# Sliding-window attention with a gated feed-forward layer: stages of batches 2 and 3 grouped in three bursts a unit, first loads, first casts and weight loads in another order

## The chip, the cores and the metric

The kernel runs on one core of one Trainium2 chip. The metric is the device time of one execution in microseconds (us); below it is given as the median of 13 runs. A profile of one execution stands beside it.

## The reference, cut to what matters

There are 4 batches, 8 heads, 768 positions, head size 64, all inputs in float32.

```python
scores = q @ k.transpose(0, 1, 3, 2) / sqrt(64)
keep = (pos_k < 4) | ((pos_q - pos_k >= 0) & (pos_q - pos_k < 128))   # 4 sinks, window of 128
a = softmax(where(keep, scores, -1e9))
x = (a @ v).transpose(0, 2, 1, 3).reshape(3072, 512)
out = (maximum(x @ w_gate, 0) * (x @ w_val)) @ w_out     # d_model 512, d_ff 1536
```

## The kernel before, in words

**Units.** Attention is done in 16 units (U0 to U15), each a pair of heads of one batch: four units to a batch. A unit loads k, q and v in float32 into one of four staging buffers (`stg`, `load_kq` L105, `load_v` L114: one DMA for k, one for q, three for v, 5 in all, some 1.2 MB), casts them to bfloat16 (`cast` L124, on GpSimd), and transposes k and q so that the head size lies on the partitions. For batches 0 and 1 TensorE does this (`T`, L140) and ScalarE copies the results out of PSUM (L153); for batches 2 and 3 two DMAs on SyncE's queue do it (`X`, L134). `sinkk` (L155) has VectorE build a second copy of some keys (`kTs`) with the four sinks in front.

Scores come in three groups (`S`, L167), each followed by an exp on ScalarE (L183) and, for batches 1 to 3, a multiplication by a mask on VectorE (L185). Batch 0 has the mask added by a matmul of a bias instead (L174). Sums and outputs come in two halves (`norm`, L253): matmuls (`V`, L187, L201), then on VectorE a transpose, a reciprocal, a transpose and a product that writes `xT` (L260 to L265). Half 0 needs score groups 0 and 1, half 1 needs groups 1 and 2.

**The feed-forward layer** goes over 96 chunks (`chunk`, L270): a batch, a half of its positions (384) and one of 12 slices of d_ff. A chunk has four gate matmuls (gp, L275), a Relu on ScalarE (L278), four value matmuls (vp, L281) and a product on VectorE (L283). When the 12 slices of a half are done, 3 x 12 matmuls with `wo` (`ffn2`, L294) are queued in `f2`; up to three of them follow each later chunk. Twelve of them make a tile that ScalarE copies (L298) and SyncE's queue stores.

**The order is written out by hand.** `unit_stages` (L360) makes six stages of a unit x: `s(0)` (with `X` of unit x+1), `v` (half 1 of unit x-1), `s(1)`, `t`, `s(2)`, and half 0 of x. Stage `t` transposes the next unit (`T`) where TensorE does it, calls `sinkk` for it, issues weight loads on GpSimd's queue and the loads of unit x+5 or x+3 on SyncE's, and casts unit x+3 on GpSimd. `held` (L328) has VectorE write one element of the staging buffer first, so that the load waits until VectorE comes there. `PLAN` (L414) says how many stages stand ahead of which chunk: 28 ahead of chunk 0, then up to 50 by chunk 24, 74 by chunk 48, 98 by chunk 71. So from chunk 24 on there is one stage ahead of about every chunk.

**Queues.** Each engine executes in the order written. GpSimd's casts and its weight loads (`load_w` L207 for gate and value, four pieces each, `load_wo` L213, three pieces of four d_ff slices) are in one line: a weight load is issued only after the casts ahead of it, and those wait for their data. SyncE's queue holds the loads of k, q, v, the transposes `X` and the stores, in the order written. The three pieces of `wo` are issued in stage `t` of units 5, 6 and 7, ahead of the casts of U8, U9 and U10.

**Buffers.** Chunks and early attention take their PSUM tiles from a pool of three (`ps_gv`), scores and later outputs from a pool of two (`ps_at`).

**The beginning** (L334 to L355): SyncE's queue gets k of U0, v of U0, then U1, U2, U3, U4; q of U0 goes to ScalarE's queue. VectorE writes the bias (`setup_m0`) and, after the cast of U0's q, `setup_m1`. GpSimd casts k and v of U0, then k, q, v of U1, U2; stage `t` of U0 issues the first weight pieces ahead of U3's casts.

Of the kernel before, what the change touches and what calls it, by code (L numbers as in the profile page):

```python
# [33 lines left out]
def kernel(  # L34
# [12 lines left out]
    nc = tc.nc  # L47
    B, H, S, D = q.shape
    assert (B, H, S, D) == (4, 8, 768, 64)
    NP = H // 2  # L50
# [21 lines left out]
    kT = [const.tile([128, 872], BF16, name=f"kT{i}") for i in range(2)]  # L72
# [15 lines left out]
    class Unit:  # L88
# [34 lines left out]

        def cast(self, what, eng):  # L124

            if what in "kq":
                eng.tensor_copy((self.kn if what == "k" else self.qn)[:],  # L127
                                self.staging(what).rearrange("p h (n d) -> p n h d", d=64))
                return
            eng.tensor_copy(self.vn[:, 0:6, :, :], self.staging("v")[:, 0:6, :, :])  # L130
            eng.tensor_copy(self.vn[0:24, 6, :, :], self.staging("v")[0:24, 6, :, :])
            eng.tensor_copy(self.vn[0:4, 1:6:2, :, :], bc(self.vn[0:4, 0, :, :], 3))
# [7 lines left out]
        def T(self, first):  # L140

            s = self.s
            if first:
                ps = ps_gv.tile([128, 1024], BF16, name="tk", tag="gv")[:]
                pq = ps_op.tile([128, 1024], BF16, name="tq", tag="op")[:]
            else:
                both = ps_at.tile([128, 2, 1024], BF16, name="tkq", tag="at")
                ps, pq = both[:, 0, :], both[:, 1, :]
            for x, p_ in ((self.kn, ps), (self.qn, pq)):
                for t in range(6):  # L150
                    nc.tensor.transpose(p_[:, t * 128:(t + 1) * 128], x[:, t, :, :].rearrange("p h d -> p (h d)"), ident[:])  # L151
            for p_, dst, cp in ((ps, kT[s], nc.scalar.copy), (pq, qT[s], nc.scalar.copy)):
                cp(dst[:, 0:S].rearrange("d (p n) -> d p n", n=6), p_[:, 0:S].rearrange("d (n p) -> d p n", n=6))  # L153

        def sinkk(self):  # L155

# [61 lines left out]
    def setup_pool():  # L218
        make_identity(nc, ident)
        t0, a = bias[:, 0:255], bias[:, 503:754]  # L220
        for x, w, d in ((t0, 255, 0), (a, 251, 4)):
            nc.gpsimd.memset(x, 0.0)
            nc.gpsimd.affine_select(out=x, in_=x, compare_op=Alu.is_ge, fill=NEG, base=d,
                                    pattern=[[1, w]], channel_multiplier=-1)
            nc.gpsimd.affine_select(out=x, in_=x, compare_op=Alu.is_ge, fill=NEG, base=127 - d,
                                    pattern=[[-1, w]], channel_multiplier=1)
# [1 line left out]
    def setup_slot(s):  # L228
        nc.vector.memset(kT[s][:, S:872], 0.0)

    cp, ms = nc.vector.tensor_copy, nc.vector.memset

    def setup_m0():

        ms(bias[0:4, 0:128], 0.0)
        ms(bias[0:4, 128:255], NEG)
        cp(bias[:, 255:503], bias[:, 503:751])
        ms(bias[0:4, 255:503], 0.0)
        ms(bias[0:4, 503:627], NEG)

    def setup_m1():

        band, sk = (lambda a, b: bias[:, 503 + a:503 + b]), (lambda n: bias[:, 255:255 + n])
        cp(bias[:, 754:1002], sk(248))
        cp(bias[:, 1002:1253], band(0, 251))
        cp(bias[:, 1253:1397], sk(144))
        cp(bias[:, 1397:1417], band(0, 20))
        nc.vector.tensor_scalar(out=msk[:], in0=bias[:], scalar1=-1.0, scalar2=None, op0=Alu.is_ge)
# [53 lines left out]
    with tc.manual_schedule():  # L302
        U = [Unit(i) for i in range(B * NP)]
        on_array = []

        def at(x):
            return U[x] if 0 <= x < len(U) else None

        def casts(u, what, eng=nc.gpsimd):
            for w in what:  # L310
                u.cast(w, eng)

        warm_ps = []

        def warm(n):

            if not warm_ps:
                warm_ps.append(ps_at.tile([128, 2, 512], F32, name="warm", tag="at"))
            for _ in range(n):
                nc.tensor.matmul(out=warm_ps[0][:, 0, 0:128], lhsT=ident[:], rhs=ident[:], start=True, stop=True,  # L320
                                 skip_group_check=True)

        def load(x):
            U[x].load_kq("k", nc.sync)
            U[x].load_kq("q", nc.sync)
            U[x].load_v(nc.sync)

        def held(x):  # L328

            if x < len(U):  # L330
                nc.vector.memset(U[x].stg[0:1, 0:1], 0.0)
                load(x)

        U[0].load_kq("k", nc.sync)  # L334
        U[0].load_kq("q", nc.scalar)
        U[0].load_v(nc.sync)
        for x in range(1, 4):
            load(x)
        nc.vector.memset(ones[:], 1.0)
        setup_pool()  # L340
        nc.scalar.activation(ee[0][:, 0, 0, 0:64], ones[:], Act.Exp, bias=0.0, scale=1.0)
        for x in range(4):
            nc.vector.memset(vn[x][:, 6, :, :], 0.0)
        setup_slot(0)
        setup_slot(1)
        setup_m0()

        warm(16)
        casts(U[0], "k")
        casts(U[0], "q", nc.vector)  # L350
        casts(U[0], "v")
        casts(U[1], "kqv")
        casts(U[2], "kqv")
        load(4)
        setup_m1()  # L355


        stages = []

        def unit_stages(x):  # L360
            u, prev, nxt = U[x], at(x - 1), at(x + 1)

            def s(gi):
                def f():
                    if gi == 0 and u.p == 0:
                        xTs[u.b] = xpool.tile([128, NP, S], BF16, name="xT")
                    if gi == 0 and nxt is not None and nxt.xbar:
                        nxt.X()
                    u.S(gi)
                return f  # L370

            def v():
                if prev is not None:
                    norm(prev, 1, ps_at if on_array else ps_gv)

            def t():
                if nxt is not None:
                    if not nxt.xbar:
                        nxt.T(not on_array)
                    nxt.sinkk()  # L380
                if x == 0:
                    load_w(0)
                    load(5)
                elif x == 1:
                    load_w(1)
                elif x == 3:
                    load_w(2)
                    load(6)
                elif x == 4:
                    load_w(3)  # L390
                    load(7)
                elif 5 <= x:
                    held(x + 3)
                    if x < 8:
                        load_wo(x - 5)
                if at(x + 3) is not None:
                    casts(at(x + 3), "kqv")
            return [s(0), v, s(1), t, s(2), lambda: norm(u, 0, ps_at if on_array else ps_gv)]

        def first():  # L400
            U[0].T(True)
            U[0].sinkk()
        stages.append(first)
        for x in range(len(U)):
            stages += unit_stages(x)
        stages.append(lambda: norm(U[-1], 1))

        si = 0
        f2 = deque()
        total = len(stages)  # L410

        ORDER = [(0, h, m) for g in range(0, FM, 3) for h in range(2) for m in range(g, g + 3)]
        ORDER += [(b, h, m) for b in range(1, B) for h in range(2) for m in range(FM)]
        PLAN = ((0, 28), (24, 50), (48, 74), (71, 98))  # L414

        def want(ci):
            for (c0, w0), (c1, w1) in zip(PLAN, PLAN[1:]):
                if ci <= c1:
                    return w0 + (w1 - w0) * (ci - c0) // (c1 - c0)
            return total  # L420
        count = {}
        n = S // 2
        for ci, (b, h, m) in enumerate(ORDER):
            if b not in hTs:
                hTs[b] = hpool.tile([128, FM, S], BF16, name="hT", tag="hT")
            while si < min(total, want(ci)):
                stages[si]()
                si += 1
            if not ci:
                on_array.append(1)  # L430
            chunk(b, h * n, n, m)
            for _ in range(min(3, len(f2))):
                f2.popleft()()
            count[b, h] = count.get((b, h), 0) + 1
            if count[b, h] == FM:
                for t in range(3 * h, 3 * h + 3):
                    for mm in range(FM):
                        f2.append(lambda b=b, t=t, mm=mm: ffn2(b, t, mm, tail=b == B - 1))
        while f2:
            f2.popleft()()  # L440
# [33 lines left out]
```

The softmax here doesn't subtract the row's maximum and nothing guards it: scores larger than these inputs give would overflow.

## Time and profile before

| | |
|---|---|
| median of 13 runs | 266.36 us (263.61 to 269.73) |
| the profiled execution's own time | 266.07 us |
| its span, first to last instruction | 264.3 us |
| mean granted TensorE clock | 0.994 |
| TensorE matmuls busy | 252.1 us (95%) |
| VectorE busy | 147.4 us (56%) |
| ScalarE busy | 115.6 us (44%) |
| GpSimd busy | 62.7 us (24%) |
| moved by DMA | 33.54 MB |

PE is TensorE, DVE VectorE, ACT ScalarE, POOL GpSimd, SP SyncE; PEld are TensorE's weight loads, and a q behind a name is the engine's queue. Matmuls overlap, so their busy time says that TensorE is held, not that it is at its peak; the starting times of neighbouring matmuls tell the pace. A row of the timeline has the start, the time taken, the engine, the line and the operation; in brackets stands the idle time ahead of it and what ended it. The waits of an engine with slack cost nothing.

### The profile page before, as it was taken

To read this page: it belongs to the slowest core of one execution; us is meant where nothing else is said; L and a number is where in the kernel's file an instruction comes from. 1 tells how busy PE (TensorE), PEld (TensorE's weight loads), DVE (VectorE), ACT (ScalarE), POOL (GpSimd) and SP (SyncE) were. 2 spreads that over 40 slices of the span, in tenths; PEclk is the share of its full clock that TensorE was granted. 3 is DMA by queue.
4 is the path that set the end of the run, shared out by engine and by line. 5 is a ranking of instruction groups with operands and counts; after the bars stand their busy time and mean duration, and the time that the engine had idled before them with its cause. 6 is when DMAs were issued, how large, how long until landed. Compare 5 with 4: busy or idle time off the path is not lost.

```text
span 264.3 us, 5141 instructions
## 1 busy us (share of the span) xinstructions
PE 252.1 (95%) x1992; PEld 139.4 (53%) x1992; DVE 147.4 (56%) x318; ACT 115.6 (44%) x186; POOL 62.7 (24%) x102
## 2 busy tenths in 40 slices
PE   3999999999968999999999999999999999999994
PEld 3555655565534555555555555555565555555441
DVE  3399969778773566665647566575656232322100
ACT  2777855646423444344344434434433323333211
POOL 5787359072323141221305050000000000000000
PEclk9999999999997999999999999999999999999999
DMA  7999999998989393939559391311011011111132
GB/s 196 313 298 228 241 240 239 226 171 144 193 131 207 91 221 20 233 89 171 111 136 183 80 203 37 66 40 42 0 42 40 0 42 40 40 42 40 40 119 79
DMA packets 77318, 33.54 MB, mean 127 GB/s; under 512 B 64496, under 2 KB 74224, under 8 KB 77296
## 3 DMA queue, kind: packets, MB, share of 16 engines
q1 hardware_dynamic: 71216, 28.12, 47.2%
q0 software_dynamic: 5808, 4.72, 11.6%
q10 hardware_dynamic: 272, 0.39, 0.4%
q8 instruction: 15, 0.25, 0.4%
q14 instruction: 7, 0.06, 0.1%
HBM read 28.51 MB, written 6.29 MB: 132 GB/s over the span
## 4 chain that ended last, share of the span: by engine, by line
PE 78%; DMA 12%; SPq 6%; POOL 1%; issue 1%; ACT 1%; DVE 0%; POOLq 0%; ACTq 0%
PE gp L275 23%; PE op L294 23%; PE vp L281 21%; PE ops L201 6%; DMA stg<-in_v_dram 5%; DMA stg<-in_q_dram 5%; PE sps L179 4%; SPq L120 3%; DMA wo<-in_moe_w_out_dram 2%; SPq L112 2%; SPq L122 1%; PE tkq L151 1%; SPq L109 0%; POOL vn L130 0%; POOL qn L127 0%
## 5 line engine op out<-in xcount | busy, mean ns | idle before, releaser
L275 PE MATMUL gp<-xT,wg 128*128 128x384 bf16 x384 | 79.3, 330 | 0.0
L281 PE MATMUL vp<-xT,wv 128*128 128x384 bf16 x384 | 78.8, 328 | 0.3 <-DVE R L260 0.3
L278 ACT ACTIVATE gs<-gp 128x384 f32<-128x384 f32 x96 | 47.1, 490 | 72.6 <-PE gp L275 72.0
L294 PE MATMUL op<-wo,hT 128*128 128x512 bf16 x288 | 75.0, 381 | 2.7 <-DMA wo<-in_moe_w_out_dram 2.7
L283 DVE TENSOR_TENSOR hT<-gs,vp 128x384 bf16<-128x384 f32 x96 | 52.8, 552 | 42.7 <-PE vp L281 40.7
L183 ACT ACTIVATE ee<-sps 128x1006 bf16<-128x1006 f32 (+2 forms) x48 | 46.2, 964 | 38.8 <-PE sps L179 38.8
L281 PEld LDWEIGHTS <-wv 128*128 128x128 bf16 x384 | 37.8, 98 | 25.9 <-issue 1.5
L275 PEld LDWEIGHTS <-wg 128*128 128x128 bf16 x384 | 32.9, 98 | 27.3 <-issue 5.1
L294 PEld LDWEIGHTS <-hT 128*128 128x128 bf16 x288 | 28.3, 98 | 26.4 <-issue 0.6
L185 DVE TENSOR_TENSOR ee<-ee,msk 128x1006 bf16<-128x1006 bf16 (+2 forms) x36 | 26.0, 721 | 29.0 <-ACT ee L183 29.0
L127 POOL CAST kn<-stg 128x768 bf16<-128x768 f32 x16 | 13.3, 829 | 61.6 <-DMA stg<-in_k_dram 45.8
L298 ACT COPY ot<-op 128x512 f32<-128x512 f32 x24 | 14.1, 586 | 26.0 <-PE op L294 26.0
L260 DVE STREAM_TRANSPOSE R<-ops 128x384 f32<-128x384 f32 x24 | 13.9, 581 | 12.2 <-PE ops L201 12.1
L130 POOL CAST vn<-stg 128x768 bf16<-128x768 f32 x16 | 14.0, 873 | 23.3 <-DMA stg<-in_v_dram 21.1
L263 DVE STREAM_TRANSPOSE R<-rc 128x384 f32<-128x384 f32 x32 | 18.5, 578 | 1.1
L265 DVE TENSOR_TENSOR xT<-ops,R 128x384 bf16<-128x384 f32 x32 | 17.8, 557 | 1.7
L179 PEld LDWEIGHTS <-kT 64*128 64x128 bf16 x128 | 6.3, 93 | 22.5 <-issue 20.5
L201 PEld LDWEIGHTS <-ones 128*64 128x64 bf16 x288 | 12.3, 109 | 10.5 <-issue 7.5
L201 PE MATMUL ops<-ee,vn 128*64 128x255 bf16 (+8 forms) x288 | 15.5, 233 | 0.3 <-DVE xT L265 0.3
L179 PE MATMUL sps<-qT,kT 64*128 64x251 bf16 (+2 forms) x128 | 15.0, 255 | 0.1
L127 POOL CAST qn<-stg 128x768 bf16<-128x768 f32 x15 | 12.5, 836 | 8.6 <-DMA stg<-in_q_dram 7.9
L179 PE MATMUL sps<-qT,kTs 64*128 64x248 bf16 (+1 forms) x96 | 12.6, 259 | 0.4 <-DVE kTs L160 0.4
(53 smaller groups left out, 131.0 us busy)
## 6 DMA issues: line engine op xcount, KB each, us to landing
stg<-in_k_dram SPq DMA_DIRECT2D x16, 384.0 KB
stg<-in_v_dram SPq DMA_DIRECT2D x32, 192.0 KB
out_dram<-ot SPq DMA_DIRECT2D x24, 256.0 KB
stg<-in_q_dram SPq DMA_DIRECT2D x15, 384.0 KB
wg<-in_moe_w_gate_dram POOLq DMA_DIRECT2D x4, 384.0 KB, 8.3
wv<-in_moe_w_val_dram POOLq DMA_DIRECT2D x4, 384.0 KB, 10.4
wo<-in_moe_w_out_dram POOLq DMA_DIRECT2D x3, 512.0 KB, 7.1
stg<-in_q_dram ACTq DMA_DIRECT2D x1, 384.0 KB
```

The lines of the kernel that those rows point to most:

```text
L127: eng.tensor_copy((self.kn if what == "k" else self.qn)[:], self.staging(what).rearrange("p h (n d) -> p n h d", d=64))
L179: nc.tensor.matmul(out=ps[:, h, c:c + w], lhsT=self.kw(j, r), rhs=qT[s][r, qa:qa + w], start=not self.biased, stop=True, skip_group_check= ...
L183: nc.scalar.activation(x, ps[:, :, 0:c], Act.Exp, bias=0.0, scale=scale)
L185: nc.vector.tensor_tensor(x, x, bc(msk[:, m0:m0 + c], 2), op=Alu.mult)
L201: nc.tensor.matmul(out=ps[1 - what][64 * h:64 * h + 64, qa - q0:qa - q0 + w], lhsT=self.vn[:, j, h, :] if what else ones[:], rhs=ee[s][:, ...
L263: nc.vector.transpose(r[:, 1, 0:w], bass.AP(a.tensor, a.offset, [a.ap[0], [1, nb], [0, 32]]))
L265: nc.vector.tensor_tensor(xTs[u.b][:, u.p, c0:c0 + w], o[:, 0:w], r[:, 1, 0:w], op=Alu.mult)
L275: nc.tensor.matmul(out=gp[:, 0:n], lhsT=wg[:, ko, m * 128:(m + 1) * 128], rhs=x[:, ko, c0:c0 + n], start=ko == 0, stop=ko == KO - 1)
L278: nc.scalar.activation(gs[:, 0:n], gp[:, 0:n], Act.Relu, bias=0.0, scale=1.0)
L281: nc.tensor.matmul(out=vp[:, 0:n], lhsT=wv[:, ko, m * 128:(m + 1) * 128], rhs=x[:, ko, c0:c0 + n], start=ko == 0, stop=ko == KO - 1)
L283: nc.vector.tensor_tensor(hT[:, m, c0:c0 + n], gs[:, 0:n], vp[:, 0:n], op=Alu.mult)
L294: nc.tensor.matmul(out=op, lhsT=hTs[b][:, m, t * 128:(t + 1) * 128], rhs=wo[:, m, :], start=m == 0, stop=m == FM - 1)
```

## The change

1. `unit_stages`: for units 8 to 15 (batches 2 and 3) the six stages become three: `v` and `s(0)`; `t` and `s(1)`; half 0 and `s(2)`, each pair issued with no chunk between. `PLAN` counts 74 stages in place of 98, in the same stretches of chunks.
2. `load_wo`: the three pieces move one stage `t` ahead, to units 4, 5 and 6.
3. The first loads: k and q of U0 and U1, then v of both, all on SyncE's queue.
4. U0's k is cast by VectorE and its q by ScalarE; GpSimd begins with k and q of U1, then v of U0 and U1. U3's casts stand ahead of the first weight pieces.
5. In U0's `T` the copies of k go to VectorE, and both k and q are copied in two halves.
6. `setup_m0` goes to GpSimd, `setup_m1` behind U0's `sinkk`.

```diff
@@ cast
+            cp = eng.copy if eng is nc.scalar else eng.tensor_copy
...
@@ T
-            for p_, dst, cp in ((ps, kT[s], nc.scalar.copy), (pq, qT[s], nc.scalar.copy)):
-                cp(dst[:, 0:S].rearrange("d (p n) -> d p n", n=6), p_[:, 0:S].rearrange("d (n p) -> d p n", n=6))
+            for a, b in ((0, 64), (64, 128)) if self.i == 0 else ((0, 128),):
+                for p_, dst, cp in ((ps, kT[s], nc.vector.tensor_copy if self.i == 0 else nc.scalar.copy), (pq, qT[s], nc.scalar.copy)):
+                    cp(dst[:, 0:S].rearrange("d (p n) -> d p n", n=6)[:, a:b, :],
+                       p_[:, 0:S].rearrange("d (n p) -> d p n", n=6)[:, a:b, :])
...
-    cp, ms = nc.vector.tensor_copy, nc.vector.memset
     def setup_m0():
+        cp, ms = nc.gpsimd.tensor_copy, nc.gpsimd.memset
...
     def setup_m1():
+        cp = nc.vector.tensor_copy
...
-        U[0].load_kq("k", nc.sync)
-        U[0].load_kq("q", nc.scalar)
-        U[0].load_v(nc.sync)
-        for x in range(1, 4):
-            load(x)
+        for x in range(2):
+            U[x].load_kq("k", nc.sync)
+            U[x].load_kq("q", nc.sync)
+        for x in range(2):
+            U[x].load_v(nc.sync)
+        load(2)
+        load(3)
         nc.vector.memset(ones[:], 1.0)
         setup_pool()
+        setup_m0()
...
-        setup_m0()
         warm(16)
-        casts(U[0], "k")
-        casts(U[0], "q", nc.vector)
+        casts(U[0], "k", nc.vector)
+        casts(U[0], "q", nc.scalar)
+        casts(U[1], "kq")
         casts(U[0], "v")
-        casts(U[1], "kqv")
+        casts(U[1], "v")
         casts(U[2], "kqv")
         load(4)
-        setup_m1()
@@ stage t
+                if x == 0:
+                    casts(at(x + 3), "kqv")
                 if x == 0:
                     load_w(0)
                     load(5)
...
                 elif x == 4:
                     load_w(3)
                     load(7)
+                    load_wo(0)
                 elif 5 <= x:
                     held(x + 3)
-                    if x < 8:
-                        load_wo(x - 5)
-                if at(x + 3) is not None:
+                    if x < 7:
+                        load_wo(x - 4)
+                if x and at(x + 3) is not None:
                     casts(at(x + 3), "kqv")
-            return [s(0), v, s(1), t, s(2), lambda: norm(u, 0, ps_at if on_array else ps_gv)]
+            def v0():
+                norm(u, 0, ps_at if on_array else ps_gv)
+
+            def both(f, g):
+                return lambda: (f(), g())
+            if x < NP:
+                return [s(0), v, s(1), t, s(2), v0]
+            return [both(v, s(0)), both(t, s(1)), both(v0, s(2))] if x >= 8 else [s(0), v, s(1), t, s(2), v0]
         def first():
             U[0].T(True)
             U[0].sinkk()
+            setup_m1()
...
-        PLAN = ((0, 28), (24, 50), (48, 74), (71, 98))
+        PLAN = ((0, 28), (24, 50), (48, 62), (71, 74))
```

## The prediction

> **What bounds the kernel.** I read the slices first, then the chain of waits, then the timeline where TensorE is not dense.
>
> The page, the second part (span in 40 slices of 6.6 us):
>
> ```profile
> span 264.3 us, 5141 instructions
> ...
> PE   3999999999968999999999999999999999999994
> ...
> PEclk9999999999997999999999999999999999999999
> DMA  7999999998989393939559391311011011111132
> ```
>
> TensorE is held from the second slice to the last, but for slices 11 to 13 (70 to 85 us), where the granted clock dips too. DMA is busy in nearly every slice up to there. So the time is: the start of the dense part, plus TensorE's work, plus that one hole. The chain of waits agrees: from 35.39 us on it is matmuls but for one piece on `wo` (73.35 us, 6.60 us) and a few us ahead of it.
>
> The hole, from the timeline of 71.5 to 102 us:
>
> ```profile
> 72.75 0.33 DVE L159 COPY kTs<-kT 128x372 bf16<-128x372 bf16 x1 [1.50 <-DMA kT<-kn]
> ...
> 73.34 0.83 DVE L283 TENSOR_TENSOR hT<-gs,vp 128x384 bf16<-128x384 f32 x1
> 73.35 0.74 POOL L214 DMA_DIRECT2D wo<-in_moe_w_out_dram  x1
> ...
> 75.36 0.82 PE L275 MATMUL gp<-xT,wg 128*128 128x384 bf16 x4
> ...
> 76.67 0.59 PE L294 MATMUL op<-wo,hT 128*128 128x512 bf16 x2
> ...
> 79.99 0.38 PE L294 MATMUL op<-wo,hT 128*128 128x512 bf16 x1 [2.72 <-DMA wo<-in_moe_w_out_dram]
> ...
> 80.62 1.46 PE L275 MATMUL gp<-xT,wg 128*128 128x384 bf16 x4
> ...
> 88.85 0.81 PE L294 MATMUL op<-wo,hT 128*128 128x512 bf16 x3
> ...
> 90.80 0.81 PE L294 MATMUL op<-wo,hT 128*128 128x512 bf16 x3
> ...
> 91.54 0.28 PE L179 MATMUL sps<-qT,kT 64*128 64x251 bf16 x2
> ```
>
> The third piece of `wo` was issued at 73.35 and TensorE had to wait for it at 77.1; behind the wait matmuls take near twice their time. The first row is VectorE waiting for U8's transposed keys: it comes back below.
>
> **The sum is made against the profiled execution**, 266.07 us (span 264.3 and 1.8 around it), 0.29 below the median of the runs.
>
> **Part 1, `wo` one stage earlier.** Three output matmuls take 0.65 us (88.85 to 89.50, the next chunk's start), 0.216 each. The third of chunk 23 was due at 76.67 + 0.43 = 77.10 and came at 79.99: 2.89 us lost. From chunk 24's first gate matmul (80.62) to the next stage (84.34) 3.72 us pass, elsewhere 1.95 + 0.09: 1.68 us lost at the lower clock (0.78 granted from 76.5 to 84.4). Together 4.57 us. In the new order the third piece stands behind U8's casts. Those ended at 61.05 before; a piece took 6.6 us to land (73.35 to 79.95), so 67.7 and 9 us early, if nothing else moved.
>
> But it does move. Piece one now follows the fourth gate and value pieces (issued 43.29 to 44.8) at once, not U7's casts (55.50). In the timeline U7's v was asked for at 39.12 and its cast began at 54.04, after 7.67 us of waiting, while the third and fourth weight pieces were moving; U6's v, asked for at 33.29 mostly behind the first four, was there at 41.37. So a load of 256-byte rows nearly stands still beside a weight piece. With `wo` queued directly behind, U8's loads (asked for at 48.14, cast 56.24 to 60.4) meet two pieces of `wo` instead of one. That puts U8's last cast between 61 (the gaps are used: DMA share 0.75 from 54 to 57 us, 0.84 from 57 to 62) and 61 + 7; I take +7 or a little more, since those gaps are small. The third piece then lands at 75 to 77, about when it is due (77.10 less the earlier start, 76.2).
>
> **What is late next** is U8's keys. SyncE's queue holds U9's loads ahead of U8's transposes (issued 69.49 and 71.31 in before). VectorE waits in `sinkk` for them (72.75), and behind it in its line stands chunk 21's product, which ended at 74.17 and frees a PSUM buffer for chunk 23's gate at 75.36: 1.19 us of slack, 0.3 once the start is 0.9 earlier. If the keys land d later, TensorE stands d - 0.3. Bounds: d = 0 (gaps absorb the pieces) and d = 7.5 (a whole piece ahead of the transposes). I take 1.5, near the low end: U8's loads come later by a piece, but U9's, asked for at 61.17 and kept to 72.7 by the second piece, then run between two pieces. Cost 1.2. Net of part 1: -3.4 us.
>
> [...]
>
> **Part 2, three bursts a unit.** A stage after output matmuls starts 0.74 us after their first (90.80 to 91.54, and 93.14 to 93.88 for sums), a chunk 0.65. So entering a stage costs 0.09, and the first gate group after it 0.01 more (0.66 and 0.65). Leaving sums and outputs costs the same whatever follows:
>
> ```profile
> 99.40 0.51 PE L201 MATMUL ops<-ee,vn 128*64 128x119 bf16 x10
> 99.85 0.34 PE L275 MATMUL gp<-xT,wg 128*128 128x384 bf16 x1
> ```
>
> ```profile
> 19.88 0.51 PE L201 MATMUL ops<-ee,vn 128*64 128x119 bf16 x10
> 20.33 0.39 PE L174 MATMUL sps<-bias,ident 128*128 128x499 bf16 x1
> ```
>
> 0.45 us to a chunk's matmul (first fence) and to a score matmul (second, from the beginning, where they do follow each other). So a score group put behind outputs saves one entry, 0.10. Before there are 5 stages with matmuls a unit (`t` has none), 40 in all, the last two together; after, 3 a unit and one at the end, 25: 15 x 0.10 = 1.5 us. Bounds: nothing (a new wait for PSUM takes it) and 2.2. VectorE gets the four steps of a half (0.58 + 0.23 + 0.58 + 0.56) and a mask product (0.7) ahead of the chunk's product (0.55): 3.2 us from the burst's start, and the buffer it frees is wanted two chunks (3.9 us) later. ScalarE's exp (1.0) and Relu (0.5) are shorter. Both are covered; if not, a few tenths at 16 places. A chunk later than before the sums need their exp: score group 2 is now two chunks ahead of half 1 in place of three, 3.9 us for exp and mask of 1.5 and VectorE's 2.0.
>
> **Part 3, the beginning.** In before ScalarE copies U0's k (6.81, 0.80) and then q (7.51 to 8.31), scores start at 8.36 and the first exp at 9.07. After, q's cast is ScalarE's (0.8, by the row of its 768-wide copies, at 5.5 when q is there) and k's copy is VectorE's; the first score group needs only the first half of q's copy, and the bias matmuls (1.05) end at about 8.0. Gain 0.4 to 0.6. U1's k and q, cast behind U0's v at 8.75 to 10.34 before, now come first, so U1's transposes at 10.38 do not hold this up. From there ScalarE's line (1.0 + 1.0 + 0.9 exps, 1.6 copies of some 5.2 us a unit, 18.4 to 28.8) carries the 0.5 on. The setup on GpSimd lies in its 1.38 us of idleness ahead of 5.07; VectorE's `setup_m1` (1.3) ends some 0.5 ahead of the second bias matmul, and costs at most that if late.
>
> Then the dense part: TensorE waited at chunk 0's values (31.90), chunk 1's, and for U5's q (34.88), which had landed at 34.0 beside the first weight pieces:
>
> ```profile
> 31.90 0.81 PE L281 MATMUL vp<-xT,wv 128*128 128x384 bf16 x4 [0.27 <-DVE R L260]
> ...
> 34.00 0.83 POOL L127 CAST qn<-stg 128x768 bf16<-128x768 f32 x1 [1.34 <-DMA stg<-in_q_dram]
> ...
> 34.88 0.51 PE L151 MATMUL tkq<-ident,qn 128*128 128x128 bf16 x6 [0.30 <-POOL qn L127]
> ```
>
> Those pieces are now behind U3's casts. The v casts stood 4.0 apart (7.29, 11.22, 15.29), so U3's at 19.3, and 1.46 later the issue (20.62 to 22.08): 20.8 against 16.75. U4's and U5's k and q run ahead of them; the 0.46 of U5's q goes. But the values' piece, issued 0.87 later, lands 10.4 us on by the median: 32.1, or 31 with less beside it. Chunk 0's values want it at 31.4: 0 to 0.7 lost. Part 3 in all: -0.9, bounds -1.3 and +0.5.
>
> **Sum:** 266.07 - 3.4 - 1.5 - 0.9 = 260.3 us.
>
> **Rivals.**
> - *Nothing is late.* The pieces fill DMA's gaps and U8's keys keep their time: 266.07 - 4.57 - 1.5 - 0.9 = 259.1. For it: DMA moved 119 GB/s from 69 to 76.5 and 131 from 57 to 62, where 221 to 257 were seen before. Against it: U7's wait.
> - *The hole comes back at the keys.* d near 3.3, and a stand of 3.0 us is as long as the one that was followed by the low clock: 259.1 + 3.0 + 1.7 = 263.8. [...]
> - *The bursts give nothing*, because VectorE holds a buffer: 261.8. For it only that VectorE's work is bunched.
> - *Slower.* The third piece gets between U9's loads and U8's transposes: the keys land 7.5 late (80.3), TensorE stands 7.2 and then 1.7 at the low clock: 259.1 + 8.9 = 268.0. It is slower from keys at about 78.4 on. Against it: the piece waits for U8's casts, and U9's loads have to run slowly at that time too.
>
> **Chances.** Forecast (259.4 to 261.5) 0.48; nothing late 0.20; hole at the keys 0.16; bursts give nothing 0.09; slower 0.07. The range 258.0 to 264.0 takes in all but the slower case, the ends of the hole and the best of all bounds. Half a per cent, 1.3 us, is about what a measurement of this kernel can tell from no change; faster by more 0.89, within 0.04, slower by more 0.07.
>
> **What would show it.** TensorE's wait on `wo` gone or under 1 us; VectorE's wait for `kT` near 72 us longer than 1.50; clock near 1.00 from 76 to 85; a unit of batches 2 and 3 taking 14.5 us where the chain shows 14.68 (87.61 to 102.29); chunk 2's gate at 34.3 (35.23). Wrong if chunk 0's values wait over 1 us, if a wait for U8's keys passes 3 us, or if vp waits for VectorE appear after 85 us.

## The result and the profile after

The kernel after takes 262.46 us by the median of 11 runs (260.88 to 263.76), the kernel before 266.46 by that of the 48 runs beside it; the ratio is 0.9882 [0.9855, 0.9909]. The profiled execution took 262.48 us (span 260.7), so it stands for the median. The runs of one kernel spread over some us: of 29 runs of the kernel before, 7 have a granted clock of 1.00 and took 262.99 to 264.83, the other 22 have 0.987 to 0.994 and took 265.07 to 270.40; each stretch below is that of one execution.

The forecast was 260.3, and the time lies in its range; of the three parts, one went better than forecast, one nearly as forecast, and the third the other way. The starts of the chunks' first gate matmuls split the two spans into the same stretches (us; before, after, difference, forecast):

| stretch | before | after | difference | forecast |
|---|---|---|---|---|
| start to chunk 2 (part 3) | 35.23 | 37.32 | +2.09 | -0.9 |
| chunk 2 to 23 | 40.13 | 40.13 | 0 | 0 |
| chunk 23 to 26, the hole (part 1) | 12.18 | 7.53 | -4.65 | -3.4 |
| chunk 26 to 71 (part 2) | 110.57 | 109.40 | -1.17 | -1.5 |
| chunk 71 to the end | 66.18 | 66.33 | +0.15 | 0 |
| sum | 264.29 | 260.71 | -3.58 | -5.8 |

The page after, the span in 40 slices of 6.5 us:

```profile
span 260.7 us, 5138 instructions
...
PE   5998889999999999999999999999999999999994
...
PEclk9999799999999999999999999999999999999999
DMA  6899999998989976748391941311011101111132
```

The dip of the clock in slice 13 of the kernel before, with TensorE not full in slices 12 and 13, is gone. A new one stands in slice 5, with TensorE not full in slices 4 to 6.

**The hole.** TensorE's timeline (start, time taken, engine, line, operation, and in brackets the idle time ahead with what ended it):

```profile
76.00 0.81 PE L297 MATMUL op<-wo,hT 128*128 128x512 bf16 x3
...
78.76 0.81 PE L297 MATMUL op<-wo,hT 128*128 128x512 bf16 x3
...
80.66 0.82 PE L278 MATMUL gp<-xT,wg 128*128 128x384 bf16 x4
...
82.61 0.81 PE L278 MATMUL gp<-xT,wg 128*128 128x384 bf16 x4
```

No bracket is left and a chunk takes 1.95 us (80.66 to 82.61), where 3.72 passed before to the next stage. The third piece of `wo` landed at 74.38. VectorE's line at the same place, where I had put what is late next:

```profile
75.67 0.35 DVE L162 COPY kTs<-kT 128x372 bf16<-128x372 bf16 x1 [2.33 <-DMA kT<-kn]
...
76.28 0.54 DVE L286 TENSOR_TENSOR hT<-gs,vp 128x384 bf16<-128x384 f32 x1
```

U8's keys came 2.9 us later than before and VectorE waited longer (2.33, before 1.50), as forecast; but the whole kernel was 2.1 us later here, and the product behind the wait still freed its buffer in time for the gate at 77.45.

**A burst**, TensorE's timeline after 88 us:

```profile
88.24 0.81 PE L297 MATMUL op<-wo,hT 128*128 128x512 bf16 x3
88.98 0.47 PE L204 MATMUL ops<-ee,ones 128*64 128x255 bf16 x8
89.31 0.45 PE L204 MATMUL ops<-ee,vn 128*64 128x255 bf16 x8
89.69 0.28 PE L182 MATMUL sps<-qT,kT 64*128 64x251 bf16 x2
...
89.98 0.82 PE L278 MATMUL gp<-xT,wg 128*128 128x384 bf16 x4
```

The entry into the stage (0.74 for three `wo` matmuls instead of 0.65) is paid once for sums, outputs and scores; before, a score group had its own (the prediction's rows at 90.80 and 91.54). From chunk 24 (80.66) to chunk 30 (95.13) it is 14.47 us a unit, where the forecast said 14.5. No vp waits for VectorE after 85 us.

**The beginning.** TensorE's timeline, then the row of its weight loads, then GpSimd's:

```profile
26.99 0.51 PE L152 MATMUL tk<-ident,kn 128*128 128x128 bf16 x6 [1.55 <-POOL kn L128]
...
29.17 0.75 PE L204 MATMUL sums<-ee,ones 128*64 128x255 bf16 x8
...
32.77 0.81 PE L278 MATMUL gp<-xT,wg 128*128 128x384 bf16 x4 [0.19 <-DVE xT L268]
34.69 0.82 PE L284 MATMUL vp<-xT,wv 128*128 128x384 bf16 x4 [1.10 <-DVE R L266]
...
37.32 0.81 PE L278 MATMUL gp<-xT,wg 128*128 128x384 bf16 x4
```

```profile
34.69 0.28 PEld L284 LDWEIGHTS <-wv 128*128 128x128 bf16 x3 [1.49 <-DMA wv<-in_moe_w_val_dram]
```

```profile
21.54 0.83 POOL L131 CAST vn<-stg 128x768 bf16<-128x768 f32 x1 [0.55 <-DMA stg<-in_v_dram]
...
23.00 0.87 POOL L213 DMA_DIRECT2D wg<-in_moe_w_gate_dram  x1
23.87 0.75 POOL L213 DMA_DIRECT2D wv<-in_moe_w_val_dram  x1
...
25.33 0.77 POOL L213 DMA_DIRECT2D wv<-in_moe_w_val_dram  x1
26.06 0.87 POOL L128 CAST kn<-stg 128x768 bf16<-128x768 f32 x1
```

The same work of GpSimd in the kernel before:

```profile
16.75 0.87 POOL L210 DMA_DIRECT2D wg<-in_moe_w_gate_dram  x1
...
20.62 0.83 POOL L130 CAST vn<-stg 128x768 bf16<-128x768 f32 x1 [0.66 <-DMA stg<-in_v_dram]
...
23.55 0.84 POOL L127 CAST kn<-stg 128x768 bf16<-128x768 f32 x1
```

From the bottom up, in the kernel after: U3's v is cast at 21.54, the four weight pieces are issued behind it, and behind those stands the cast of U4's k, for which TensorE waits 1.55 us at 26.99 (0 before). The value piece issued at 23.87 lands at 34.64, and chunk 0's values wait for it. The matmul row names VectorE, which had read the sums by 33.80; the weight load's row names the DMA. The first exp does come earlier (8.03, before 9.07) and the lead holds to 23.86 (24.87), where these two waits take it.

DMA moved less early on. Windows of four us, of the kernel before and of the kernel after; the last three columns are the granted clock, the DMA share and GB/s:

```profile
8.00:12.00 4.00, 3.89 (x25) 1.94 (x24) 0.37 (x2) 2.83 (x4) 3.12 (x7) 1.00 1.17 300
```

```profile
8.00:12.00 4.00, 3.84 (x30) 1.84 (x30) 0.72 (x3) 3.52 (x5) 2.93 (x5) 1.00 0.79 164
...
28.00:32.00 4.00, 4.00 (x49) 2.62 (x48) 3.52 (x5) 2.76 (x4) 2.68 (x5) 0.57 1.24 189
```

The last row is the new dip: 0.57 of the clock for four us behind the stall, in which eight sums matmuls take 0.75 in place of 0.47.

### The profile page after: what moved, and what is told of

It is laid out like the page before. It is cut to its first block, busy times and chain, and to the rows that moved or that the text cites. A ratio compares the mean times of both kernels' runs of the same rounds, so it can differ in the third digit from the quotient of the medians.

```text
span 260.7 us, 5138 instructions
## 1 busy us (share of the span) xinstructions
PE 250.0 (96%) x1992; PEld 140.1 (54%) x1992; DVE 146.8 (56%) x315; ACT 116.2 (45%) x187; POOL 61.6 (24%) x106
## 4 chain that ended last, share of the span: by engine, by line
PE 88%; DMA 5%; DVE 2%; POOL 1%; ACT 1%; issue 1%; SPq 1%; ACTq 0%; DVEq 0%; POOLq 0%
PE gp L278 25%; PE vp L284 24%; PE op L297 24%; PE ops L204 7%; DMA stg<-in_q_dram 5%; PE sps L182 5%; PE tkq L152 1%; PE sps L177 1%; DVE kTs L163 1%; SPq L112 1%; PE tq L152 1%; DVE R L266 0%; ACT ee L186 0%; DVE R L263 0%; PE tk L152 0%
## 5 line engine op out<-in xcount | busy, mean ns | idle before, releaser
L278 PE MATMUL gp<-xT,wg 128*128 128x384 bf16 x384 | 78.5, 327 | 0.2 <-DVE xT L268 0.2
L278 PEld LDWEIGHTS <-wg 128*128 128x128 bf16 x384 | 34.0, 98 | 30.1 <-issue 4.9
L128 POOL CAST kn<-stg 128x768 bf16<-128x768 f32 x15 | 12.5, 831 | 53.1 <-DMA stg<-in_k_dram 30.4
L128 POOL CAST qn<-stg 128x768 bf16<-128x768 f32 x15 | 12.5, 831 | 11.3 <-DMA stg<-in_q_dram 10.4
L182 PEld LDWEIGHTS <-kT 64*128 64x128 bf16 x128 | 6.2, 94 | 13.6 <-issue 10.4
```

Source lines behind the costliest of these rows:

```text
L128: cp((self.kn if what == "k" else self.qn)[:], self.staging(what).rearrange("p h (n d) -> p n h d", d=64))
L182: nc.tensor.matmul(out=ps[:, h, c:c + w], lhsT=self.kw(j, r), rhs=qT[s][r, qa:qa + w], start=not self.biased, stop=True, skip_group_check= ...
L278: nc.tensor.matmul(out=gp[:, 0:n], lhsT=wg[:, ko, m * 128:(m + 1) * 128], rhs=x[:, ko, c0:c0 + n], start=ko == 0, stop=ko == KO - 1)
```

## The experiments

Two theories stood at first for the late beginning. G: GpSimd's line; U3's casts put ahead of the weight issues make these late, and U4's casts later still. L: the order of the loads; with k and q of two units first and then six v loads in a row DMA stands partly idle, and U2's and U3's v come late. Two runs check parts 1 and 2. All medians are of 6 to 12 runs; the kernel before took 266.6 to 267.1 beside them. Where the intervals of two ratios overlap, a difference is read from the timelines, each of one execution.

**1. The first weights ahead of U3's casts again** (all else as after).

```diff
                 if x == 0:
-                    casts(at(x + 3), "kqv")
-                if x == 0:
                     load_w(0)
...
-                if x and at(x + 3) is not None:
+                if at(x + 3) is not None:
```

> After, with U3's casts back behind the first weight pieces on GpSimd's queue. Theory G (GpSimd's line: U4's casts stand behind U3's v and four weight issues in a row, 23.00 to 26.06 us, so U4's transposes come 1.55 us late, the clock drops, and the first value piece lands only at 34.6): the wait for U4's k and the one for the value piece go, chunk 2's gate starts at about 34.3 us instead of 37.3, and the whole is about 259.5 us, unless U8's keys or wo now make TensorE stand around 76 us. Theory L (the load order: six loads of v in a row leave DMA partly idle from 9 to 12 us and bring U2's and U3's v 1 to 2 us later): U3's v still comes at 21.5, chunk 2's gate at 36.5 or later, the whole 261.5 or more.

263.76 us, ratio 0.9957 [0.9917, 0.9998]: slower than after. Chunk 0 comes at 30.58, as G had it, but chunk 2 only at 38.51. The profiled execution took 265.37, the longest of the twelve and 1.6 over their median, so the waits below are as long as they get; what is read from them is their order. GpSimd's rows, then TensorE's and SyncE's queue:

```profile
34.11 0.83 POOL L131 CAST vn<-stg 128x768 bf16<-128x768 f32 x1 [7.37 <-PE vp L284]
...
36.18 0.82 POOL L128 CAST kn<-stg 128x768 bf16<-128x768 f32 x1 [0.56 <-DMA stg<-in_k_dram]
```

```profile
37.06 0.51 PE L152 MATMUL tkq<-ident,kn 128*128 128x128 bf16 x6 [3.05 <-POOL kn L128]
```

```profile
20.79 4.20 SPq L112 DMA_DIRECT2D stg<-in_k_dram  x1
...
26.31 4.75 SPq L120 DMA_DIRECT2D stg<-in_v_dram  x2
```

The 7.37 us are put down to a matmul, but what came last is U4's v: asked for from 18.8 on, its pieces landed at 29.84, 33.97 and 34.39, beside four weight pieces whose parts landed from 23.6 to 35.6. U5's k, behind it in both lines, landed at 36.06. SyncE's queue sat 4.20 us on one issue and 4.75 on two. So the wait changes places: late weights make chunk 0's values wait, early ones U4's v and with it U5's k. Theory G alone falls.

**2. The loads in the order of before** (all else as after).

```diff
-        for x in range(2):
-            U[x].load_kq("k", nc.sync)
-            U[x].load_kq("q", nc.sync)
-        for x in range(2):
-            U[x].load_v(nc.sync)
-        load(2)
-        load(3)
+        U[0].load_kq("k", nc.sync)
+        U[0].load_kq("q", nc.scalar)
+        U[0].load_v(nc.sync)
+        for x in range(1, 4):
+            load(x)
```

> After, with the first loads in the order and on the queues of before (k of U0 and its v on SyncE's, q of U0 on ScalarE's, then unit by unit), the casts as in after. Theory L: U3's v is there at 19.3 instead of 21.5, U4's casts start 1.5 to 2 us earlier, chunk 2's gate at about 35, the whole about 260.5 us. Theory G: the four weight issues in a row still stand ahead of U4's casts and the value piece still comes late, chunk 2's gate at 36.5 or later, the whole 261.5 to 262.5; the first exp, at 8.03 in after, may be later by some tenths.

261.03 us, ratio 0.9862 [0.9808, 0.9916]. Chunk 2 at 35.90, 1.42 sooner than after; from 8 to 12 us DMA moves 300 GB/s again, U2's v is cast at 15.30 (17.94), U4's k at 25.09 (26.06), and no low clock is seen. Chunk 2 lies between L's 35 and G's 36.5. The ratio's interval overlaps that of the kernel after, so by time alone the gain isn't shown; run 9 against run 8 shows it again. GpSimd's row of U3's v:

```profile
20.56 0.83 POOL L131 CAST vn<-stg 128x768 bf16<-128x768 f32 x1 [2.14 <-DMA stg<-in_v_dram]
```

It comes at 20.56, as it did in before (20.62), though no weight piece stands ahead of it here.

**3. `wo` one stage earlier, alone** (the kernel before with the two lines of `load_wo` of the change).

> Before, with the three pieces of wo issued one stage earlier and nothing else. If the hole at 77 us was wo and the low clock behind it alone: the 4.6 us go and the whole is about 261.9 us (ratio 0.983). If U8's transposed keys are the next to be late when the start is not late too (in after they landed at 75.65 instead of 72.73, and the start came 2.1 later): TensorE stands 1 to 3 us at chunk 23 and the whole is 263 to 264.5.

262.20 us, ratio 0.9900 [0.9865, 0.9936]: part 1 alone gives as much as the whole change. The hole is gone (chunk 23 at 75.01, chunk 26 at 82.64: 7.63 us). VectorE's wait for the keys in this kernel:

```profile
73.56 0.31 DVE L159 COPY kTs<-kT 128x372 bf16<-128x372 bf16 x1 [2.66 <-DMA kT<-kn]
```

They came 0.8 later than before (72.75), within the 1.19 of slack, and TensorE did not stand. The granted clock is 0.997 or more in all twelve runs.

**4. After without the bursts** (`unit_stages` returns six stages, `PLAN` as before).

> After, with the six stages of a unit and the old plan for batches 2 and 3. If a merged stage saves one entry (0.1 us at 15 places): 1.2 to 1.5 us more than after, 263.6 to 264 us. If the bursts cost as much as they save by a new wait: the same as after, 262.5. The start and the stretch to chunk 23 stay as in after.

263.58 us, ratio 0.9952 [0.9908, 0.9997], 1.1 over after; chunk 26 to 71 takes 110.56, as before (110.57). So the bursts are worth 1.16 here, and nothing takes it. Another 0.10 of theirs lies in the stretch of the hole, 7.63 us in runs 3 and 4 and 7.53 in the kernel after.

**5. The base of the following runs.** In these, k and q of batches 2 and 3 are moved but not transposed.

```diff
-                nc.sync.dma_start_transpose(out=dst[:, 0:S].rearrange("d (t r) -> d t r", r=128),
-                                            in_=x[:].rearrange("r t h d -> r (t h d)"))
+                nc.sync.dma_start(out=dst[:, 0:S], in_=x[:].rearrange("r t h d -> r (t h d)"))
```

> The kernel after, but DMA carries k and q of batches 2 and 3 over as they lie, without transposing them (that part of the computation is left out; the DMAs, casts and waits keep their places). It is the base of the runs that have the same left out. Expected, since no wait for transposed keys stood on the path: the kernel after's course, chunk 2's first gate matmul at 37.3, chunk 26 at 85.0, in all 262.0 to 262.6 us. If it is faster by 0.5 us or more, the transposes cost time somewhere that the chain of waits did not name.

262.26 us, chunk 2 at 37.52: the course of the kernel after. What is left out does not carry its time. TensorE waits for U4's k here too, but the clock does not drop:

```profile
27.15 0.51 PE L151 MATMUL tk<-ident,kn 128*128 128x128 bf16 x6 [1.47 <-POOL kn L128]
```

```profile
28.00:32.00 4.00, 3.06 (x56) 2.23 (x58) 3.36 (x5) 2.77 (x4) 2.84 (x5) 1.00 1.25 191
```

The clock is 1.00 where the kernel after has 0.57, and chunk 2 comes no sooner (37.52, after 37.32). So the dip is not what makes the beginning late.

**6. The beginning of before, with the earlier `wo` and the bursts.**

> As the base (k and q of batches 2 and 3 not transposed), with the whole beginning of the kernel before; wo one stage earlier and the three bursts are kept. It prices the start edits by themselves. Theory 1 (they cost what the trace shows, 2.09 us at chunk 2, and nothing later gives it back): chunk 2 at 35.0 to 35.3, chunk 26 at 82.7 to 83.0, in all 1.4 to 2.1 us under the base. Theory 2 (a later wait takes the earlier start back): under 0.7 us.

260.81 us, by medians 1.45 under the base, as theory 1 had it. By the means of the six runs it is only 0.7, which is theory 2's, because two of them took 263. (One of these two was profiled, 263.45; in it U5's k and q made TensorE wait 1.18 and 0.83 us and chunk 2 came at 36.35.) So this run alone does not settle the price. Runs 3 and 4 do, with twelve runs each and the transposes in place: both have the earlier `wo` and no bursts, and they differ in the start edits alone. They took 262.20 and 263.58, so the start edits cost 1.4 us (by the means 1.4 too, give or take 0.6).

**7. Only the second pair of weight pieces one stage later.**

```diff
-                elif x == 1:
+                elif x == 2:
                     load_w(1)
```

> As the base, with one edit: the second pair of weight pieces one stage later. U4's k cast comes 1.5 us sooner (24.6 instead of 26.06). Theory G (U4's casts behind the issues make the late start, through the stall of TensorE and the low clock after it): transposes of U4 at 25.5 to 26, no dip of the clock, chunk 0 at 30.8 to 31.3, chunk 2 at 35.5 or sooner, 1.5 us or more under the base. Theory V (the values' piece alone sets it, since its issue stays at 23.9): the piece still lands at 34, or at 33 with nothing of the second pair beside it; chunk 0's values wait from 31.5 on, chunk 2 at 36.0 to 37.3, at most 1.2 us under the base.

263.08 us (262.4 without its two longest runs): no gain over the base, 262.26. U4's transposes came sooner (25.76), as G wanted, but the value piece, issued at 24.06, landed at 35.41 and chunk 0's values waited for it:

```profile
35.46 0.13 PEld L283 LDWEIGHTS <-wv 128*128 128x128 bf16 x2 [1.99 <-DMA wv<-in_moe_w_val_dram]
```

(The profiled execution took 265.07, one of the two longest, so only the order of events is read from it.) Theory V fits, by the time and by this order: the position of the first pair is enough to make the beginning late. With these few runs the time alone only just speaks against G's 1.5.

**8. Three edits together:** the loads of before (run 2), the first pair ahead of U3's casts (run 1), the second pair later (run 7).

> As the base, with three edits at the beginning: the loads in the order of before; the first pair of weight pieces issued ahead of U3's casts, as before; the second pair one stage later, ahead of U5's casts (its pieces are first wanted by chunk 6, near 42 us). Theory B (the beginning is bound by DMA bytes and by GpSimd's one line, and the second pair stands in both for nothing): the first pieces land by 29.5, chunk 0's values do not wait, U4's v and U5's k have no second pair beside them; chunk 0 at 30.0 to 30.6, chunk 2 at 33.8 to 34.6, in all 2.7 to 3.5 us under the base. Theory H (U5's casts now stand behind the second pair's issue, 1.5 us): the wait for U5's k goes on as in the run with w0 ahead, chunk 2 at 35.5 or later, under 1.8 us. If the second pair is late instead, chunk 6's gate waits for wg near 42 us.

259.46 us (259.07 to 259.91), ratio 0.9748 [0.9706, 0.9790], 2.8 under the base, as theory B had it. TensorE's timeline:

```profile
30.22 0.81 PE L277 MATMUL gp<-xT,wg 128*128 128x384 bf16 x4
31.31 0.81 PE L283 MATMUL vp<-xT,wv 128*128 128x384 bf16 x4 [0.27 <-DVE R L262]
...
33.49 0.50 PE L151 MATMUL tkq<-ident,kn 128*128 128x128 bf16 x6
...
34.16 0.81 PE L277 MATMUL gp<-xT,wg 128*128 128x384 bf16 x4
```

Neither wait is left: not the values (the piece landed at 27.73) and not U5's k (33.49, no bracket). U4's v was there at 28.60, where run 1 had 34.39. The second pair stood in the way of both and is not missed: chunk 6 comes at 41.92 without a wait.

**9. As run 8, but with the loads in the new order.**

> As the base (k and q of batches 2 and 3 not transposed), with the first pair of weight pieces ahead of U3's casts and the second pair one stage later, but the loads in the new order. Against the run with the old loads (chunk 2 at 34.16, 259.46 us) it tells the order of the loads by itself; against the run with w0 ahead and both pairs early (chunk 2 at 38.51) the second pair by itself. Theory B (the second pair beside U4's v and U5's k made the wait; the order of the loads costs the 1.4 us that it cost before, or less): chunk 0 at 30.5 to 31.0, chunk 2 at 34.7 to 35.6, 260.0 to 260.9 us. Theory L (the order of the loads alone keeps U4's v and U5's k late): chunk 2 at 36.5 or later, 261.8 us or more.

261.27 us, 1.8 over run 8; chunk 2 at 36.22, between the two theories and outside what I expected of either. Windows:

```profile
8.00:12.00 4.00, 3.63 (x38) 1.72 (x36) 0.93 (x4) 3.56 (x5) 3.08 (x6) 1.00 0.94 189
```

So both count: against run 1 the second pair is worth 2.3 us at chunk 2 (2.5 by the medians), and the order of the loads 2.1 against run 8 (1.8 by the medians; 1.4 in run 2).

**10. As run 6, with the second pair later** (the first casts, copies and setup of before).

> The base with the whole beginning of the kernel before (as in the run that had it), and one edit: the second pair of weight pieces one stage later. From the fastest run so far it differs only in the first casts, copies and setup, which are here on the engines of before: first exp at 9.1 instead of 8.6. If these edits are worth the 0.4 to 0.6 us that was predicted for them: chunk 0 at 30.2 to 30.8, chunk 2 at 34.6 to 35.0, 259.9 to 260.1 us. If the lead is lost again in a queue behind them: chunk 2 at 34.0 to 34.4, 259.3 to 259.6 us. If U5's k stays late for another reason than the second pair, chunk 2 stands at 35 to 36.4 as in the run with the old beginning.

259.98 us, chunk 2 at 34.67: 0.5 behind run 8 in both. So the first casts and copies on idle engines give what was forecast for them, once nothing behind them takes it. (One of its six runs took 263.55, so the times alone would not show it; the starts of chunk 2 do.)

**11. As run 9, with the loads mixed.**

```diff
-        for x in range(2):
+        for x in range(4):
             U[x].load_v(nc.sync)
-        load(2)
-        load(3)
+            if x < 2:
+                U[x + 2].load_kq("k", nc.sync)
+                U[x + 2].load_kq("q", nc.sync)
```

> As the run with w0 ahead, the second pair later and the new loads (261.27 us, chunk 2 at 36.22; k and q of batches 2 and 3 not transposed), but with the first loads mixed: k and q of U0 and U1 first, as in the new order, then v of U0, k and q of U2, v of U1, k and q of U3, v of U2, v of U3. If six v loads in a row are what starves DMA in the new order (164 to 189 GB/s from 8 to 12 us against 300): DMA moves 250 GB/s or more from 8 to 12 us, chunk 2 at 34.2 to 35.2, 259.5 to 260.4 us. If the new order is slow because U1's k and q ahead put U0's v, U2 and U3 later in themselves: chunk 2 at 35.8 or later, 260.9 us or more.

263.10 us, chunk 2 at 37.08: a miss in time. Windows:

```profile
8.00:12.00 4.00, 3.83 (x40) 1.72 (x36) 0.66 (x3) 3.31 (x5) 3.00 (x5) 1.00 1.02 298
...
16.00:20.00 4.00, 3.29 (x46) 2.03 (x48) 1.71 (x6) 2.52 (x4) 2.75 (x6) 1.00 0.95 217
```

The gap of 8 to 12 us is gone, but one appears at 16 to 20 (303 in before), where now the v of U2 and of U3 stand in a row: in both orders the thin stretch comes where two v's stand in a row. Why the time is worse is only read from GpSimd's line: it casts U1's v ahead of U2's k, that v now comes behind U2's k and q (waits of 1.95 and 1.25 us for v of U1 and U2), and U2's transposes move from 14.91 in run 9 to 16.44. This run changed two things at once, so the share of the v's in a row in the 1.8 us of the load order is not settled.

## Why the prediction was right in its range and wrong in one of its three parts

The time lies in the stated range but outside the band that the forecast gave itself, 259.4 to 261.5. Part 1 went 1.25 us better than forecast, part 2 0.3 worse and part 3 3.0 worse. The range was made wide for a hole at the keys; that it took in a loss at the beginning instead is luck.

**Part 1** was right and larger than forecast. The 2.89 us of waiting and the 1.68 of low clock went whole (4.57 worked out; the stretch is 4.55 shorter in run 3, and 4.65 with the bursts). The term that failed is the one set against it: "If the keys land d later, TensorE stands d - 0.3 ... I take 1.5 ... Cost 1.2." Run 3, with the start nearly as before, measured d at 0.8 and a stand of 0. The bound at 0 was the better one here, as the first rival had it. The third piece landed at 74.38 against the "75 to 77".

**Part 2** was right in mechanism, too large in size: "15 x 0.10 = 1.5 us" measured 1.17 in the kernel after and 1.16 against run 4; with the 0.10 in the stretch of the hole it is 1.27, or 0.085 an entry. No buffer was held.

**Part 3** failed, by 3.0 us in the profiled executions (+2.09 for -0.9). The step is "The v casts stood 4.0 apart (7.29, 11.22, 15.29), so U3's at 19.3, and 1.46 later the issue (20.62 to 22.08): 20.8 against 16.75." The cast came at 21.54 and the issue at 23.00. I had taken the 1.3 us between 19.3 and before's 20.62 for the price of the weight piece beside it; run 2 has no piece ahead and still 20.56, so that was mis-sized from the start. The other 1.0 is the order of the loads, which I had counted only as an earlier k and q, not as a later v for U2 and U3. The landing "10.4 us on by the median" held: 10.8. So the value piece landed 2.5 us past the forecast's 32.1, 2.2 of it by the later issue, and the condition that was to show the forecast wrong, "if chunk 0's values wait over 1 us", came true at 1.49.

A second thing is missing from the step: I moved an issue behind U3's casts and counted who gains (U4's and U5's loads run ahead of the weights), but not who stands behind the issues now. All four pieces, 3 us of GpSimd's line, then stood as one block ahead of U4's k. "The 0.46 of U5's q goes" was right, and U4's 1.55 came in its place. Taken away alone, in run 7, it gives nothing: TensorE then waits for the weights instead.

What was right in part 3: the first exp's lead, 0.4 to 0.6, is 0.56 in run 8 against run 10 (8.58, 9.14), and chunk 2 keeps 0.51 of it. In the kernel after, with the new loads as well, the lead was 1.04. All start edits together cost 1.4 (run 4 against run 3); by runs 1, 2, 7 and 8 their causes hang together: of the edits taken one at a time, only the loads (2) help, the two weight issues (1, 7) don't, and all three together give 2.8, with no overlap of the single runs (run 8 at most 259.91, run 5 at least 261.14).

**The rivals.** 262.46 lies between "the bursts give nothing" (261.8) and "the hole comes back at the keys" (263.8), and neither happened. "Nothing is late" was right for the keys and wrong for the time. No rival had the beginning as the loss; its bound of +0.5 was too tight, because it bounded the landing of the piece and not the issue.

**A faster beginning** is that of run 8, 259.46. That kernel leaves out the transposes of k and q of batches 2 and 3; no run has this beginning together with them. The base and the kernel after agree in time (262.26, 262.46), but in run 8 VectorE waits 2.61 us for U8's keys at 72.79, three us earlier than they came in the kernel after, and whether transposed keys keep that time is open.

## What to carry to other kernels

When an issue is moved behind other work in a queue, follow it both ways: to its landing, and to what now stands behind it in the same queue. Check the assumed time of what it waits for in a kernel or a place where the suspected cause is absent. Weights that are wanted 20 us later do not belong in the first rush (the second pair there cost 2.3 us at chunk 2, run 1 against run 9), and a change of load order is priced by the load that comes last in it (here U2's v, cast at 17.94 in place of 15.30), not by the one that comes first.

## What the runs showed of the hardware that was not expected

- A stall of 1.55 us (25.4 to 27.0) was followed by a clock of 0.50 from 29 to 31 us; in run 1, behind a stand of 3.05, it was 0.52 from 38 to 40; in run 6, behind stands of 1.18 and 0.83, it was 0.62 from 36 to 38 and 0.53 from 38 to 40. Runs 2 and 8, without such stalls, kept 1.00; but so did run 5 behind 1.47 and run 11 behind 1.34 (16.44). So in these runs the length of the stall alone does not tell whether a low clock follows.
- Where two units' v loads (rows of 256 bytes) stand in a row, DMA moved 159 to 233 GB/s over four us (164 in the kernel after, 233, 159 and 189 in runs 1, 5 and 9, from 8 to 12 us; 217 in run 11, from 16 to 20), where with k, q and v by turns it moved 300 to 305 from 8 to 20 us (before, runs 2 and 8). SyncE's issue of one such load, a tail of 12 KB, took 2.82 us in the kernel after (4.46 to 7.28).
- VectorE's copy of 128x12 elements took 1.95 us at 28.76 in the kernel after, and 0.15 to 0.42 at the 15 other places there; in the kernel before it took 0.15 to 1.18. GpSimd's casts stood without a break beside the long one (26.06 to 30.68). No run shows the cause.
- Of the first weight piece issued on GpSimd's queue the first of its 16 parts landed 4.9 us (run 8, 17.48 to 22.39), 5.3 us (after, 23.87 to 29.15) and 5.6 us (before, 17.62 to 23.23) behind the end of the issue, and the rest in another 2.3 to 2.7. The value piece behind it in the kernel after had its first part 7.3 us behind its issue (24.61 to 31.94) and the rest in 2.7. So in these kernels most of the time to its landing passed before any of it was there.
